# A chunked delta rule: inverses by row operations on VectorE instead of doubling on TensorE, state accumulated in PSUM, selected rows fetched by an indirect DMA

## The chip, the cores and the metric

The kernel runs on one core of one Trainium2 chip. The metric is the device time of one execution in microseconds (us). Besides the times there is one profiled execution, whose trace gives each engine's instructions: TensorE (PE, and PEld for its weight loads), VectorE (DVE), ScalarE (ACT), GpSimd (POOL), and the DMA issues of SyncE (SP).

## The reference

Two blocks follow each other, all in fp32. The first is the delta rule for 4 batches, 8 heads, 768 tokens and head size 48:

```python
k_n = k / (np.linalg.norm(k, axis=-1, keepdims=True) + 1e-06)
for t in range(S):
    y[:, :, t] = q_t @ state
    v_old = kn_t @ state
    state = state + beta_t * outer(kn_t, v_t - v_old)
```

The second is a mixture of depths on x = y with the heads joined (4 x 768 x 384). Each token's score is x . w_gate; in each batch the 128 tokens with the highest scores get x + sigmoid(score) * (relu(x w1) w2), with an inner size of 1024; the other tokens keep x.

## The kernel before

Tokens are taken in chunks of 64. In a chunk, with kn the normalised keys, S the state ahead of it and L[t, s] = beta_s kn_t.kn_s for s < t:

```
W = (I + L)^-1 (V - kn S)      Y = Q S + strict(Q (beta kn)^T) W      S <- S + (beta kn)^T W
```

A step is one chunk of two batches: 16 heads, stacked two by two on the 128 partitions (8 pairs). There are 24 steps, 12 for the first two batches (a group), then 12 for the other two.

`invert(i)` does what needs no state: keys are normalised (ACT, DVE, POOL), keys and queries are turned by TensorE (p_t, L236), the two 64x64 Gram matrices of a head are formed (p_g, L246) and masked. The inverse T = (I + L)^-1 then comes by doubling (L272 to L287): for blocks of 2, 4, 8, 16 and 32, p_x = L T (L262, masked on DVE at L275), p_ttt and p_tt (L262) give the corrections to T^T and T, which DVE subtracts (L281, L285). Each product is 16 matmuls of 64x64; the trace shows two MATMUL instructions for each, as fp32 products have. `recur(i)` then does the part that needs the state: p_r = kn S (L306), the difference on DVE (L309), p_w = T r (L316), its copy by ACT (L320), p_s (L330) and its addition to the state on DVE (L333), and the outputs p_y (L348, L354). `depths(g, ...)` is the second block for a group: a ranking by counting on DVE, a selection matrix, gathering the selected rows by 36 matmuls a batch (L442), two layers (L455, L464) and an indirect DMA that adds the result to the output.

All of these are generators. A loop at the end of the program advances them in turn, so an inverse runs two steps ahead of its recurrence; depths(0) is spread among the steps of the second group, and depths(1) comes after everything else. The Tile framework fixes each engine's order of instructions when the program is built; an engine then runs them in that order.

## Time and profile before

| | us |
|---|---|
| median of 3 runs (lowest, highest) | 770.15 (770.09, 771.6) |
| span of the profiled execution | 769.4 |
| PE busy | 704.5 |
| DVE busy | 391.0 |
| POOL busy | 146.5 |
| ACT busy | 139.8 |

The profiled execution's span, from its first to its last instruction, lies 0.75 us below the median of the timed runs; nothing else lies around it. Busy times are sums over an engine's instructions without overlap. Matmuls are pipelined, so the mean duration of one MATMUL (some 220 ns) is a latency; what one costs in a stream is the busy time of its group divided by its count.

### The profile page before, as it was taken

Reading aid. Unit: us, or ns where it says so; the run is one execution under the profiler, and the core shown is the slowest. Engines: PE = TensorE matmul, PEld = TensorE weight load, DVE = VectorE, ACT = ScalarE, POOL = GpSimd, SP = SyncE. Lnnn points to the kernel's source line nnn. Section 1 sums busy time; section 2 is a strip of 40 time slices with the busy share of each in tenths; the row PEclk is TensorE's granted clock in tenths of the full one; section 3 lists DMA queues with packets and bytes.
Section 4 is the critical chain, followed back from the end, with each engine's and each line's share of the span. In section 5 each row is a group of like instructions: output and inputs, shape, how many; then the busy total and the mean of one; then the engine's idle time right before and its main releaser. Section 6 shows DMA issues by size and latency. Waiting matters only on the chain.

```text
span 769.4 us, 35403 instructions
## 1 busy us (share of the span) xinstructions
PE 704.5 (92%) x16740; PEld 649.5 (84%) x16740; DVE 391.0 (51%) x788; ACT 139.8 (18%) x283; POOL 146.5 (19%) x154
## 2 busy tenths in 40 slices
PE   3799999999999999999989999999999999983496
PEld 2689899999989999998888888889999999972484
DVE  3466555654655555555845942345554654546500
ACT  3022121221112112212113122111120111101011
POOL 5322022202220222113201120222121210101001
PEclk9999999999999999999979999999999999995679
DMA  7621111110211112202101110121110000000001
GB/s 123 190 45 34 35 34 35 45 34 14 54 24 35 34 25 43 44 14 50 28 13 23 33 23 13 27 50 23 29 35 9 24 4 3 24 3 22 0 1 20
DMA packets 82210, 25.38 MB, mean 33 GB/s; under 512 B 76944, under 2 KB 81680, under 8 KB 82064
## 3 DMA queue, kind: packets, MB, share of 16 engines
q1 hardware_dynamic: 81488, 22.33, 13.5%
q8 instruction: 131, 2.15, 1.2%
q0 software_dynamic: 576, 0.79, 0.8%
q14 instruction: 15, 0.12, 0.1%
HBM read 17.60 MB, written 5.51 MB: 30 GB/s over the span
## 4 chain that ended last, share of the span: by engine, by line
PE 80%; DVE 10%; DMA 3%; POOL 2%; issue 2%; ACT 1%; SPq 1%; POOLq 0%; ACTq 0%; DVEq 0%
PE p_ttt L262 15%; PE p_x L262 14%; PE p_tt L262 10%; PE p_t L236 5%; PE p_g L246 5%; PE p_y L354 4%; PE p_y L348 4%; DVE junk_r L410 4%; PE p_s L330 3%; PE p_m L455 3%; PE p_t L262 3%; PE p_w L316 3%; PE p_m L442 3%; PE p_r L306 3%; DMA k_raw<-in_k_dram 2%; PE p_m L464 2%
## 5 line engine op out<-in xcount | busy, mean ns | idle before, releaser
L262 PE MATMUL p_x<-tt,lt 64*64 64x64 f32 x3840 | 139.9, 222 | 9.5 <-DVE tt L285 8.5
L262 PE MATMUL p_ttt<-ttt,x 64*64 64x64 f32 x3840 | 139.9, 222 | 5.1 <-DVE x L275 4.8
L281 DVE TENSOR_TENSOR ttt<-ttt,p_ttt 128x512 f32<-128x512 f32 x120 | 82.4, 687 | 118.5 <-PE p_ttt L262 118.5
L262 PEld LDWEIGHTS p_x<-tt,lt 64*64 64x64 f32 x3840 | 124.5, 136 | 21.0 <-DVE tt L285 15.1
L262 PEld LDWEIGHTS p_ttt<-ttt,x 64*64 64x64 f32 x3840 | 123.6, 136 | 15.0 <-DVE x L275 7.5
L275 DVE TENSOR_TENSOR x<-lmask,p_x 128x512 f32<-128x512 f32 x120 | 82.4, 686 | 99.5 <-PE p_x L262 97.6
L262 PE MATMUL p_tt<-x,ttt 64*64 64x64 f32 x3072 | 106.9, 219 | 0.0
L262 PEld LDWEIGHTS p_tt<-x,ttt 64*64 64x64 f32 x3072 | 98.9, 136 | 0.0
L285 DVE TENSOR_TENSOR tt<-tt,p_tt 128x512 f32<-128x512 f32 x96 | 65.8, 685 | 16.8 <-PE p_tt L262 16.6
L220 POOL TENSOR_TENSOR kn<-k_raw,rn 128x384 f32<-128x384 f32 x24 | 19.9, 827 | 252.2 <-PE p_t L236 243.3
L320 ACT COPY wbd<-p_w 64x384 f32<-64x384 f32 x48 | 22.7, 473 | 160.7 <-PE p_w L316 160.1
L348 PE MATMUL p_y<-s,qt 48*64 48x48 f32 x704 | 48.9, 220 | 0.0
L223 POOL TENSOR_TENSOR bmask<-mask_u,beta_t 128x512 f32<-128x512 f32 x24 | 25.5, 1064 | 120.2 <-DVE pt L249 119.8
L348 PEld LDWEIGHTS p_y<-s,qt 48*64 48x64 f32 x704 | 45.1, 137 | 0.0
L354 PE MATMUL p_y<-wbd,pt 128*64 128x96 f32 x384 | 43.2, 255 | 1.1 <-ACT wbd L320 1.1
L255 POOL TENSOR_TENSOR ttt<-lt,m 128x512 f32<-128x512 f32 x24 | 33.9, 1410 | 27.5 <-DVE lt L249 27.5
L354 PEld LDWEIGHTS p_y<-wbd,pt 128*64 128x64 f32 x384 | 33.7, 138 | 4.8 <-ACT wbd L320 1.2
L237 ACT COPY kt<-p_t 48x512 f32<-48x512 f32 x48 | 25.6, 578 | 62.9 <-PE p_t L236 62.9
L226 POOL TENSOR_TENSOR kb<-kn,beta_t 128x384 f32<-128x384 f32 x24 | 19.9, 828 | 89.4 <-PE p_s L330 89.2
L330 PE MATMUL p_s<-wbd,kb 128*48 128x96 f32 x352 | 34.1, 249 | 0.0
L333 DVE TENSOR_TENSOR s<-s,p_s 48x384 f32<-48x384 f32 x40 | 21.8, 546 | 23.0 <-PE p_s L330 20.8
L364 DVE CUSTOM_DVE_ANT_0 junk<-x,wg 128x384 bf16<-128x384 f32 x24 | 23.1, 964 | 20.1 <-ACT x L361 20.1
(95 smaller groups left out, 833.7 us busy)
## 6 DMA issues: line engine op xcount, KB each, us to landing
k_raw<-in_k_dram SPq DMA_DIRECT2D x48, 96.0 KB, 3.0
q_raw<-in_q_dram SPq DMA_DIRECT2D x48, 96.0 KB, 3.0
v_raw<-in_v_dram SPq DMA_DIRECT2D x48, 96.0 KB, 2.9
out_dram<-x SPq DMA_DIRECT2D x24, 192.0 KB, 1.9
w_sb<-in_moe_w_dram SPq DMA_DIRECT2D x2, 1536.0 KB, 12.1
wg<-in_moe_w_gate_dram SPq DMA_DIRECT2D x1, 192.0 KB, 6.1
beta_sb<-in_beta_dram SPq DMA_DIRECT2D x2, 48.0 KB, 2.7
out_dram<-oe,idx POOLq DMA_INDIRECT x4, 4.4
```

The source lines that it names most:

```text
L236: nc.tensor.transpose(ps[:D, r * P:(r + 1) * P], x[:, r0 + r], ident)
L237: nc.scalar.copy(xt[:, r0:r0 + 4].rearrange("d r t -> d (r t)"), ps[:D])
L246: nc.tensor.matmul(ps[hs, r], lhsT=kt[:, r, hs], rhs=x[:, r, hs], start=True, stop=True)
L255: nc.gpsimd.tensor_tensor(out=ttt, in0=lt, in1=bc(m1), op=ALU.mult)
L262: nc.tensor.matmul(ps[hs, r], lhsT=lhsT[hs, r], rhs=rhs[hs] if rhs is ident2 else rhs[hs, r], start=True, stop=True)
L275: nc.vector.tensor_tensor(out=x, in0=bc(lmask[s]), in1=ps, op=ALU.mult)
L281: nc.vector.tensor_tensor(out=new, in0=ttt, in1=ps_a, op=ALU.subtract)
L285: nc.vector.tensor_tensor(out=new, in0=tt, in1=ps_b, op=ALU.subtract)
L330: nc.tensor.matmul(ps[:, r], lhsT=m["kb"][:, bb * HP + r], rhs=wb[:, bb * HP + r], start=True, stop=True)
L348: nc.tensor.matmul(y[rows, h * D:(h + 1) * D], lhsT=m["qt"][:, r, par * C:(par + 1) * C], rhs=s_old[:, r, par], start=(h == 0), stop=False ...
L354: nc.tensor.matmul(y[rows, r * 2 * D:(r + 1) * 2 * D], lhsT=m["pt"][:, bb * HP + r], rhs=wb[:, bb * HP + r], start=(c == 0 and r == 0), st ...
L410: nc.vector.tensor_scalar(out=junk[:, :e - a], in0=rows[:, a:e], scalar1=mine, scalar2=None, op0=op, op1=ALU.add, accum_out=count[:, j, o: ...
```

## The change

The part that needs no state is now `prep` for a chunk (a unit: still one chunk of two batches). Heads of the two batches sit at partitions 0 to 47 and 64 to 111 of kq and kn, padded to 64, so one transpose serves two heads, and matmuls of the two batches use different row halves of the PE array. Beta is no longer folded into keys but into the inverse.

The inverse is now made for four chunks at once (`eliminate(e)`, six calls). The 64x64 matrices are split in half; each 32x32 diagonal block becomes one partition's 1024 numbers (128 blocks, 128 partitions) through a DVE transpose, and DVE inverts all of them with 30 row operations of two instructions each, on (31 - j) x j elements for j = 1 to 30. `join(e)` then makes the lower left quarter by two products of 32x32 blocks (p_z, p_j), copied by ACT. Two SBUF to SBUF DMAs a unit and two a call put blocks where they are needed. Calls of `eliminate` for the next four chunks are advanced among the units.

In `recur` the state stays in PSUM over all chunks of a group (p_s): the new product accumulates there, and ACT copies the sum out. The score of a token is now formed by a product on POOL and a sum on ACT. In `depths` the selected rows come by an indirect DMA from the output and three transposes a batch instead of 36 matmuls. Loads of k, q and v are cut in four DMAs instead of two, and beta is read by 96 small DMAs, issued on ACT's queue ahead of ACT's first computation. Eight units are prepared and the first call of `eliminate` is finished before the first recurrence.

The diff, cut to its core (removed lines are mostly those of the functions above):

```diff
+    BC = 4
+    NB = BC * GP
+    NE = NG * NCH // BC
+    assert NB == HC
+    DP = 64
...
+    KB = 3
+    qraw = [const.tile([P, HP, GB, DP], FP32, name=f"q_raw{m}") for m in range(KB)]
+    NKN = 9
+    kns = [const.tile([P, HP, GB, DP], FP32, name=f"kn{m}") for m in range(NKN)]
+        g, c = units[i]
+        if name == "q":
+            t = qraw[i % KB]
...
+            for bb in range(GB):
+                r0 = (g * GB + bb) * HP
+                nc.sync.dma_start(
+                    out=dst[par * C:(par + 1) * C, bb],
+                    in_=src[name][par, c * C:(c + 1) * C, r0:r0 + HP])
...
+    for g in range(NG):
+        for e in range(NCH // BC):
+            for par in range(2):
+                for half in range(2):
+                    for c in range(BC):
+                        p0 = (par * 2 + half) * HC + c * GP
+                        for r in range(1):
+                            nc.scalar.dma_start(
+                                out=bt[p0:p0 + GP, g * (NCH // BC) + e],
+                                in_=beta_src[par, half, g, e, c])
+    nbt = const.tile([P, NE, HC], FP32, name="nbt")
...
+    def prep(i):
+        g, c = units[i]
+        e, m = divmod(i, BC)
...
+        kn = kns[i % NKN]
+        for bb in range(GB):
+            nc.gpsimd.tensor_tensor(
+                out=kn[:, :, bb, :D], in0=kr[:, bb], op=ALU.mult,
+                in1=rn[:, bb * HP:(bb + 1) * HP, None].to_broadcast([P, HP, D]))
+        yield
+        kq = keep.tile([P, HP, 2, P], FP32, name="kq")
+        for o, x in ((1, qr), (0, kn)):
+            ps = ps_inv("p_t")
+            for r in range(HP):
+                nc.tensor.transpose(ps[:, r * P:(r + 1) * P],
+                                    x[:, r].rearrange("p b d -> p (b d)"), ident)
+            nc.scalar.copy(kq[:, :, o], ps.rearrange("p (r t) -> p r t", t=P))
+            yield
+        ps = [ps_inv("p_g").rearrange("p (r t) -> p r t", t=P) for bb in range(GB)]
+        for r in range(HP):
+            for bb, par in order:
+                ds = slice(bb * DP, bb * DP + D)
+                hs = slice(par * C, (par + 1) * C)
+                nc.tensor.matmul(ps[bb][hs, r], lhsT=kq[ds, r, 0, hs],
+                                 rhs=kq[ds, r, :, hs], start=True, stop=True)
+        pt = keep.tile([P, HP, GB, C], FP32, name="pt")
+        gv = gs[e][:, m * GP:(m + 1) * GP].rearrange("p (r b) t -> p r b t", b=GB)
+        for bb in range(GB):
+            nc.scalar.copy(gv[:, :, bb], ps[bb][:, :, :C])
+            nc.vector.tensor_tensor(
+                out=pt[:, :, bb], in0=ps[bb][:, :, C:], op=ALU.mult,
+                in1=mask_u[:, None, :].to_broadcast([P, HP, C]))
+        for par in range(2):
+            hs = slice(par * C, par * C + HC)
+            ms = slice(m * GP, (m + 1) * GP)
+            nc.sync.dma_start(out=gs[e][hs, ms, HC:], in_=gs[e][hs, ms, :HC])
+        made[i] = dict(kn=kn, kq=kq, pt=pt)
+    def eliminate(e):
+        gt = gs[e]
+        a = work.tile([P, HC, HC], FP32, name="a")
+        tmp = work.tile([P, HC * HC // 4], FP32, name="a_tmp", bufs=1)
+        nc.vector.transpose(out=a, in_=gt[:, :, HC:].rearrange("p n t -> p t n"))
+        yield
+        nc.vector.tensor_tensor(out=a, in0=a, op=ALU.mult,
+                                in1=nbt[:, e, :, None].to_broadcast([P, HC, HC]))
+        nc.gpsimd.affine_select(out=a, in_=a, pattern=[[1, HC], [-1, HC]], base=0,
+                                channel_multiplier=0, compare_op=ALU.is_gt, fill=0.0)
+        nc.gpsimd.memset(a.rearrange("p i c -> p (i c)")[:, ::HC + 1], 1.0)
+        yield
+        for j in range(1, HC - 1):
+            w = HC - 1 - j
+            t = tmp[:, :w * j].rearrange("p (i c) -> p i c", c=j)
+            nc.vector.tensor_tensor(
+                out=t, op=ALU.mult,
+                in0=a[:, j + 1:, j:j + 1].to_broadcast([P, w, j]),
+                in1=a[:, j:j + 1, :j].to_broadcast([P, w, j]))
+            nc.vector.tensor_tensor(out=a[:, j + 1:, :j], in0=a[:, j + 1:, :j],
+                                    in1=t, op=ALU.add)
+            yield
+        nc.vector.tensor_tensor(out=a, in0=a, op=ALU.mult,
+                                in1=bt[:, e, None, :].to_broadcast([P, HC, HC]))
+        yield
+        tt = tts[e % NTT]
+        nc.vector.transpose(out=tt[:, :, HC:].rearrange("p n t -> p t n"), in_=a)
+        for par in range(2):
+            hs = slice(par * C, par * C + HC)
+            nc.sync.dma_start(out=tt[hs, :, :HC], in_=tt[hs, :, HC:])
+        yield
+        nc.vector.transpose(out=gt[:, :, HC:].rearrange("p n t -> p t n"),
+                            in_=a.rearrange("p i c -> p c i"))
+        yield
+        yield from join(e)
+    def join(e):
+        gt, tt = gs[e], tts[e % NTT]
+        for m in range(0, BC, 2):
+            n0 = m * GP
+            lo = [slice(par * C, par * C + HC) for par in range(2)]
+            hi = [slice(par * C + HC, (par + 1) * C) for par in range(2)]
+            ns = slice(n0, n0 + 2 * GP)
+            ps = ps_inv("p_z").rearrange("p (n t) -> p n t", t=HC)
+            for b in range(2 * GP):
+                for par in range(2):
+                    nc.tensor.matmul(
+                        ps[lo[par], b], lhsT=gt[hi[par], n0 + b, :HC],
+                        rhs=tt[hi[par], n0 + b, HC:], start=True, stop=True)
+            for par in range(2):
+                nc.scalar.activation(gt[lo[par], ns, :HC], ps[lo[par]], AF.Copy,
+                                     scale=-1.0)
+            yield
+            ps = ps_inv("p_j").rearrange("p (n t) -> p n t", t=HC)
+            for b in range(2 * GP):
+                for par in range(2):
+                    nc.tensor.matmul(
+                        ps[lo[par], b], lhsT=gt[lo[par], n0 + b, HC:],
+                        rhs=gt[lo[par], n0 + b, :HC], start=True, stop=True)
+            for par in range(2):
+                nc.scalar.copy(tt[lo[par], ns, HC:], ps[lo[par]])
...
+    p_s = psum.tile([P, HP, 2 * D], FP32, name="p_s")
+    nc.vector.memset(p_s, 0.0)
...
+        ps = psum.tile([P, 2, 512], FP32, name="p_r", tag="rec", bufs=1)
+        pr = ps[:, :, :HP * D].rearrange("p b (r d) -> p b r d", d=D)
+            for r in range(HP):
+                for bb, par in order:
+                    ds = slice(bb * DP, bb * DP + D)
+                    hs = slice(par * C, (par + 1) * C)
+                    nc.tensor.matmul(pr[hs, bb, r], lhsT=kq[ds, r, 0, hs],
+                                     rhs=s_old[ds, r, par], start=True, stop=True)
...
-            s_new = state.tile([D, GP, 2, D], FP32, name="s")
-            for bb in range(GB):
-                ps = ps_rec("p_s")[:D, :HP * 2 * D].rearrange(
-                    "p (r h d) -> p r h d", h=2, d=D)
-                rs = slice(bb * HP, (bb + 1) * HP)
-                for r in range(HP):
-                    nc.tensor.matmul(ps[:, r], lhsT=m["kb"][:, bb * HP + r],
-                                     rhs=wb[:, bb * HP + r], start=True, stop=True)
-                if c > 0:
-                    nc.vector.tensor_tensor(out=s_new[:, rs], in0=s_old[:, rs],
-                                            in1=ps, op=ALU.add)
-                else:
-                    nc.vector.tensor_copy(s_new[:, rs], ps)
+            for r in range(HP):
+                for bb in range(GB):
+                    nc.tensor.matmul(p_s[bb * DP:bb * DP + D, r],
+                                     lhsT=kn[:, r, bb, :D],
+                                     rhs=wb[:, bb, r].rearrange("p h d -> p (h d)"),
+                                     start=(c == 0 and r == 0), stop=True,
+                                     skip_group_check=True)
+            s_new = sts[i % 2]
+            nc.scalar.copy(s_new.rearrange("p r h d -> p r (h d)"), p_s)
...
+                xw = work.tile([P, DM], FP32, name="xw", bufs=1)
+                nc.gpsimd.tensor_tensor(out=xw, in0=xj, in1=wg, op=ALU.mult)
+                nc.scalar.activation(junk, xw, AF.Copy,
+                                     accum_out=tok[b][:, j, 1:2])
...
+            xe = moe.tile([CAP, DM], FP32, name="xe")
+            nc.gpsimd.indirect_dma_start(
+                out=xe, out_offset=None, in_=out_flat[:(b + 1) * S, :],
+                in_offset=bass.IndirectOffsetOnAxis(ap=idx[b][:, 0:1], axis=0))
+            xes[b] = xe
+            yield
+        for b in bs:
+            ps = ps_inv("p_m")
+                nc.tensor.transpose(ps[:, t * CAP:(t + 1) * CAP],
+                                    xes[b][:, t * P:(t + 1) * P], ident[:CAP, :CAP])
...
-                for j in range(NT):
-                    nc.tensor.matmul(ps[:, t * CAP:(t + 1) * CAP],
-                                     lhsT=xs[b][:, j, t * P:(t + 1) * P],
-                                     rhs=sel[b][:, j],
-                                     start=(j == 0), stop=(j == NT - 1))
...
+    for i in range(BC):
+        start_prep(i)
+        if i == 1:
+            load_weights()
+        finish("prep")
+    ensure(0, "v")
+    ensure(1, "v")
+    running["elim"] = eliminate(0)
+    for i in range(BC, 2 * BC):
+        start_prep(i)
+        for _ in range(8):
+            advance("prep")
+            advance("elim")
+        finish("prep")
+    finish("elim")
+    TICKS = 10
+    for i in range(n):
+        e, m = divmod(i, BC)
+        if m == 0:
+            finish("elim")
+            if e + 1 < NE:
+                running["elim"] = eliminate(e + 1)
+        ensure(i + 2, "v")
+        running["rec"] = recur(i)
+        if i == NCH:
+            running["moe"] = depths(0)
+        start_prep(i + 2 * BC)
```

## Rows read from the trace of the kernel before

**Rows 1.** The page's busy times: engine, busy us (share of span), instructions
```profile
PE 704.5 (92%) x16740; PEld 649.5 (84%) x16740; DVE 391.0 (51%) x788; ACT 139.8 (18%) x283; POOL 146.5 (19%) x154
```

**Rows 2.** Three stretches: us; busy us of PE, PEld, DVE, ACT, POOL; PEclk; DMA
```profile
20.00:40.00 20.00, 15.11 (x305) 13.83 (x303) 9.03 (x17) 2.48 (x6) 6.83 (x7) 1.00 0.59 170
...
100.00:200.00 100.00, 99.84 (x2688) 94.25 (x2685) 54.37 (x96) 18.96 (x40) 18.68 (x19) 1.00 0.16 33
...
680.00:700.00 20.00, 14.39 (x280) 12.20 (x274) 6.72 (x12) 3.70 (x7) 2.72 (x2) 0.81 0.06 22
```

**Rows 3.** Groups of PE instructions: shapes, count | busy us, mean ns | idle
```profile
L262 PE MATMUL p_x<-tt,lt 64*64 64x64 f32 x3840 | 139.9, 222 | 9.5 <-DVE tt L285 8.5 <-ACT tt L269 0.7
...
L262 PE MATMUL p_tt<-x,ttt 64*64 64x64 f32 x3072 | 106.9, 219 | 0.0
...
L348 PE MATMUL p_y<-s,qt 48*64 48x48 f32 x704 | 48.9, 220 | 0.0
...
L354 PE MATMUL p_y<-wbd,pt 128*64 128x96 f32 x384 | 43.2, 255 | 1.1 <-ACT wbd L320 1.1
L330 PE MATMUL p_s<-wbd,kb 128*48 128x96 f32 x352 | 34.1, 249 | 0.0
...
L236 PE MATMUL p_t<-ident,q_raw 128*48 128x128 f32 x192 | 26.2, 281 | 3.3 <-DVE beta_t L170 3.3
...
L455 PE MATMUL p_m<-xeT,w_sb 128*128 128x256 f32 x96 | 23.1, 389 | 0.6 <-ACT xeT L446 0.6
...
L464 PE MATMUL p_m<-w_sb,hT 128*128 128x384 f32 x64 | 21.3, 489 | 0.0
```

**Rows 4.** Groups of DVE, ACT and POOL instructions, same columns
```profile
L281 DVE TENSOR_TENSOR ttt<-ttt,p_ttt 128x512 f32<-128x512 f32 x120 | 82.4, 687 | 118.5 <-PE p_ttt L262 118.5
...
L364 DVE CUSTOM_DVE_ANT_0 junk<-x,wg 128x384 bf16<-128x384 f32 x24 | 23.1, 964 | 20.1 <-ACT x L361 20.1
...
L320 ACT COPY wbd<-p_w 64x384 f32<-64x384 f32 x48 | 22.7, 473 | 160.7 <-PE p_w L316 160.1
...
L237 ACT COPY qt<-p_t 48x512 f32<-48x512 f32 x48 | 25.5, 578 | 25.6 <-PE p_t L236 25.5
...
L220 POOL TENSOR_TENSOR kn<-k_raw,rn 128x384 f32<-128x384 f32 x24 | 19.9, 827 | 252.2 <-PE p_t L236 243.3 <-DVE rn L216 8.9
...
L211 DVE TENSOR_REDUCE rn<-ksq 128x8 f32<-128x384 f32 x24 | 13.2, 549 | 9.6 <-ACT ksq L209 9.5
...
L423 DVE TENSOR_TENSOR sel<-iota_r,rank 128x768 f32<-128x768 f32 x4 | 3.8, 958 | 0.1
```

**Rows 5.** Timeline, two p_x products of 32 instructions: start us, us
```profile
26.50 1.97 PE L262 MATMUL p_x<-tt,lt 64*64 64x64 f32 x32 [0.68 <-ACT tt L269]
...
33.73 1.15 PE L262 MATMUL p_x<-tt,lt 64*64 64x64 f32 x32 [0.79 <-DVE tt L285]
```

**Rows 6.** DMA issues: a load pair in the timeline, the stores, the indirect ones
```profile
30.71 1.27 SPq L96 DMA_DIRECT2D k_raw<-in_k_dram  x2
...
L362 SPq DMA_DIRECT2D out_dram<-x x24: 332/338/572, 97.5 to 694.5; - x24
...
DMA to landing us min/median/max: 1.9/1.9/4.2
...
out_dram<-oe,idx POOLq DMA_INDIRECT x4, 4.4
```

**Rows 7.** Timeline at the recurrence's end and in the tail
```profile
691.67 2.27 PE L354 MATMUL p_y<-wbd,pt 128*64 128x96 f32 x16 [1.12 <-ACT wbd L320]
...
693.85 1.47 POOL L379 TENSOR_TENSOR diag<-ident,tok 128x768 f32<-128x768 f32 x1 [34.82 <-DVE tok L364]
...
694.49 1.25 DVE L364 CUSTOM_DVE_ANT_0 junk<-x,wg 128x384 bf16<-128x384 f32 x1 [0.71 <-ACT x L361]
...
713.03 5.77 PE L442 MATMUL p_m<-sel,x 128*128 128x128 f32 x36
...
734.71 6.82 PE L442 MATMUL p_m<-sel,x 128*128 128x128 f32 x36
```

More of the change, by code (lines that the diff above doesn't have):

```diff
@@ L17 @@
 C = 64
+HC = 32
 @with_exitstack
@@ L156, in bc @@
[L156 to L160 removed]
+    mask_u = const.tile([P, C], FP32, name="mask_u")
+    for par in range(2):
+        hs = slice(par * C, (par + 1) * C)
+        nc.gpsimd.affine_select(out=mask_u[hs], in_=ones[hs, :C], pattern=[[1, C]],
+                                base=0, channel_multiplier=-1,
+                                compare_op=ALU.is_gt, fill=0.0)
@@ L173 @@
+    tts = [const.tile([P, NB, C], FP32, name=f"tt{m}") for m in range(NTT)]
+    for t in tts:
+        nc.gpsimd.memset(t, 0.0)
     iota_r = const.tile([P, CAP], FP32, name="iota_r")
@@ L287, in invert @@
             yield
-        made[i] = dict(kb=kb, kt=kt, qt=qt, pt=pt, ttt=ttt)
-    xs, st_g, p_y = {}, {}, {}
+    st_g, p_y = {}, {}
+    p_s = psum.tile([P, HP, 2 * D], FP32, name="p_s")
+    nc.vector.memset(p_s, 0.0)
+    sts = [const.tile([P, HP, 2, D], FP32, name=f"s{m}") for m in range(2)]
     def recur(i):
-        g, c = steps[i]
+        g, c = units[i]
+        e, ch = divmod(i, BC)
         m = made.pop(i)
+        kq, kn, pt, tt = m["kq"], m["kn"], m["pt"], tts[e % NTT]
         vr = raw.pop((i, "v"))
@@ L472, in depths, with advance @@
             yield
-    def ps_alone():
-        return psum.tile([P, 512], FP32, name="p_m", tag="m", bufs=1)
-    HALF = 9
-    AHEAD = 2
-    n = len(steps)
-    load(0, "v")
-    for i in range(1, AHEAD + 1):
-        for name in "kqv":
-            load(i, name)
-    load_weights()
-    running = {}
-    def advance(key):
-        gen = running.get(key)
-        if gen is not None and next(gen, running) is running:
-            del running[key]
+    running = {}
+    def advance(key, times=1):
+        for _ in range(times):
+            gen = running.get(key)
+            if gen is not None and next(gen, running) is running:
+                del running[key]
     def finish(key):
```

283 lines of the change are left out of this document (88 added, 195 removed).

## The prediction, made before the changed kernel was run

> **What bounds the kernel now.** I read the page's busy times first, then stretches by the window, then the groups of instructions, last the timeline of the end. PE is busy 704.5 of 769.4 us and DVE half as long [rows 1]. In the stretch from 100 to 200 us PE is busy 99.84 of 100 us at a granted clock of 1.00 [rows 2]: a step there costs what its matmuls cost, and waits of others are covered. Most of PE's time is the doubling: p_x 139.9 us, p_ttt as much with the same count, p_tt 106.9 [rows 3]. That is 36 ns an instruction; the 768 of the first transpose (p_t, L262) at this price are 28 more. So 415 of the 704.5 us belong to work that the change takes from TensorE.
>
> The pace of PE can be read closer in the timeline: 32 instructions of one product span 1.15 us, the last one's own latency of 0.22 included, so one starts every (1.15 - 0.22) / 31 = 30 ns; at 26.5 us the same product took 1.97 us, 56 ns each [rows 3, 5]. These products alternate between two quarters of the array. Where consecutive matmuls stay in one quarter the price is 48.9 / 704 = 70 ns (p_y, L348, 48 columns); with 96 columns and all 128 rows it is 97 (p_s) to 112 ns (p_y, L354) [rows 3].
>
> The end matters too: the last output product ends at 691.67 + 2.27 = 693.9 us, and 75.5 us of second block follow with nothing beside them [rows 7].
>
> **The change: PE's share of a unit.** All fp32 products are two instructions each, transposes one.
> - Turning keys and queries: 8 instructions instead of 16, 26.2 / 192 = 0.136 us each [rows 3]: 1.1 us.
> - Gram products: 32 instructions instead of 64, 128 columns wide. No row shows this form. From below each costs the pace of 30 ns: 1.0 us. From above I extend the line from 70 ns (48 columns) to 112 (96 columns) to 140 ns at 128 columns and let two run side by side: 2.2 us. I take 1.7, since the four quarters are all used.
> - p_r and p_w: 32 each at 30 ns, 1.0 us each.
> - p_s: 16, now in two column halves of the array in turn: between 16 x 97 = 1.55 us [rows 3] and half of it, 0.8. I take 1.0.
> - p_y from the state: 32, now alternating row halves within one column half: 1.0 (30 ns) to 2.2 us (70 ns), I take 1.5. p_y from W: 16 x 112 ns, 1.8 us, as before.
> - join: 256 instructions in four units, 64 x 30 ns = 1.9 us.
>
> Low, taken, high: 9.7, 11.0, 12.8 us a unit, where 769.4 us now hold 24 steps. The trace shows two quarters in turn at 30 ns against 70 in one [rows 3, 5]. [...]
>
> **DVE's share.** Two groups give its price: 512 elements 687 ns, 768 elements 958 ns [rows 4], so 1.06 ns an element and 145 ns fixed. The row operations are 60 instructions on 2 x 4960 elements: 60 x 0.145 + 9920 x 0.00106 = 19.2 us. Three transposes and two products of 1024 elements are 1.23 us each at this price (transposes on DVE have no row; below, half of it, above, twice): 6.2. One call is 25.4 us, 6.35 a unit. prep adds 0.55 (the reduce, [rows 4]), three small ones and two masks of 256 elements: 1.85; the difference in recur 0.55. Together 8.75 us. What goes: five levels of three instructions of 0.69 us.
>
> To this comes POOL. The score's product on DVE reads two SBUF operands; by the price above 384 elements are 0.55 us, but its mean is 0.96 [rows 4], and at 694.49 it took 1.25 us beside POOL's diag, which ran from 693.85 to 695.32 [rows 7]. All row operations have two SBUF operands. POOL's work in a unit is 2 x 0.41 for kn (half of L220 each, [rows 4]), 0.83 for the score and a quarter of one select of 1024 elements (2.2 us at L220's price): 2.2 us. DVE is thus at 8.75 to 11 us a unit, nearly even with PE. ACT has some six instructions of 0.5 us more than one step had, and stays at about 6 us.
>
> **The chain of the recurrence in a unit:** p_r 1.15, difference 0.55, p_w 1.15, two copies of 0.47 in turn [rows 4], p_s 1.0 to 1.55, one copy of 0.5 for the state: 5.7 to 6.3 us with hops. It is covered as long as PE has prep and join to do.
>
> So neither PE (11) nor DVE (up to 11) nor the chain (6) fills a unit alone; instructions don't yield to each other, and orders are fixed beforehand. I take 13 us for the 16 units with a prep beside them, 9.5 for the four with only an eliminate (PE 8.2, DVE 8.3), 7.5 for the last four (chain 6, PE 6.3). 208 + 38 + 30 = 276. depths(0) adds its two layers to PE, (23.1 + 21.3) / 2 = 22 us [rows 3]: 298 us. With 11 us a unit where I take 13 (and 8 and 6.5 later) it would be 256.
>
> **The start**, which has no cover. ACT issues 96 DMAs ahead of its first computation. SP's issue of a load (512 pieces) takes 1.27 / 2 = 0.64 us, that of a store (128 pieces) 0.34 [rows 6]; one of 8 pieces lies on that line at 0.24. Ends 23 and 61 us; I take 0.34: 32, with the first instruction and a landing of 1.9 us [rows 6] ACT begins at 35 us. Behind it waits the first Square and so everything. The first prep: about 2.6 us of small steps on ACT, DVE and POOL, 4.5 on PE at the slow pace [rows 5], 1.3 for copies, 3 for the DMA of the block: 11.5. Three more behind it at PE's 4.5: 25 in all. Then the first eliminate, 25.4 plus 2.2 for POOL's select, with four preps' 1.85 on the same DVE: 35. Then join for the first two units, two products of 64 instructions at 56 ns and two copies of 0.58 each time [rows 4, 5]: 9.5. The recurrence begins at 105 us. Two loads in place of one on SP cost nothing here: they hide behind ACT's issues; without that cover they'd be 0.34 us each.
>
> **The tail.** 75.5 us now. The two groups of gather matmuls go, 5.77 us ahead of the second batch's ranking and 6.82 ahead of the layers [rows 7]. In place of the second stand an indirect DMA (4.4 us from issue to landing for those of before, [rows 6]) and three transposes, 5.2 us; the first is covered by the second batch's ranking. The score goes through POOL and ACT, 0.8 us more than DVE alone. PE will have waited for the gather and starts the layers at the slow pace of [rows 5]: I add 2.5 us, between nothing and the 8 us that the first layer's 11.5 us would cost more at 1.7 times the price. 75.5 - 12.6 + 5.2 + 0.8 + 2.5 = 71 us. Stores and gathers of the same rows are ordered by DMA waits, which fall on POOL's and SP's queues while these have nothing else.
>
> **Sum:** 105 + 298 + 71 = 474 us of span, with the 0.75 between span and median 475 us.
>
> **Rivals.**
> 1. *Waits bind the unit.* DVE's row operations stand in a fixed order with the difference that the recurrence waits for, and PE waits with it. At 17 us a unit (12 and 10 later, 30 for depths(0)) the middle is 390 us, the total 567. For it: three engines within 11 us of each other, each also waiting for another. Against: the present program keeps PE at 99.84 of 100 us with as many hand-overs [rows 2].
> 2. *The slow clock.* From 680 to 700 us PE was busy 14.39 of 20 us and the granted clock was 0.81; from 20 to 40 it was busy 15.11 us, with p_x still at 1.97 us at 26.5 [rows 2, 5]. PE at 11 of 13 us is not far above. At 1.97 / 1.15 = 1.7 times PE's price a unit is some 21 us (15 and 12 later, 38 for depths(0)): 482, total 661. Against: at that pace PE would be busy nearly all the time, as from 100 to 200 us, where the clock was 1.00. [...]
> 3. *Slower than before: row operations that wait for POOL each time.* If E is one eliminate, the total is (80 + E) + (5 E + 73) + 72, with E once in the start and five times bound by DVE. It passes 770 at E = 91 us, when a row operation costs (91 - 6) / 60 = 1.4 us instead of 0.32. That is what the score's product paid beside a running POOL instruction [rows 7], for every one of 60; but POOL works 2.2 us in a unit.
>
> **Chances:** forecast 0.60 (417 to 555: start 92 to 135, middle 256 to 340, tail 68 to 79), rival 1 0.20, rival 2 0.15, rival 3 0.05. The range 420 to 625 leaves out most of rivals 2 and 3 and the forecast's lowest edge. A change under 0.2% is about what a measurement of this kernel can't tell from none: faster 0.95, within it 0.01, slower 0.04.
>
> **What would show it.** ACT's first Square at about 35 us; the first p_w at 105; DVE's row operations at 0.32 us on average; p_x, p_ttt, p_tt gone and PE at some 340 us; units 13 us apart up to the 16th; p_g below 70 ns an instruction; about 71 us from the last p_y to the end. Wrong if ACT's issues cost twice as much, if PE's clock falls in the middle, or if DVE idles ahead of the difference while PE idles behind it.

## The result and the profile after

The changed kernel takes 534.86 us (median of 4, 534.48 to 538.1) against 770.22 (median of 4) for the kernel before: ratio 0.694, 95% interval 0.6912 to 0.6969. Its profiled span is 532.8 us. The first two lines are the page's busy times of the changed kernel, the third TensorE's granted clock in 40 slices.

```profile
PE 322.5 (61%) x5652; PEld 273.4 (51%) x5652; DVE 264.5 (50%) x722; ACT 166.8 (31%) x378; POOL 84.6 (16%) x126
...
PEclk9999999555569959965975576699969758856599
```

PE has lost 382 of the 704.5 us of [rows 1], but it is no longer the engine that everything waits for: 61% busy, and its granted clock, 1.00 where [rows 2] show the doubling, is mostly between 0.5 and 0.9 in a slice. Stretches of the changed kernel follow: one for each of the start's phases (first four), then one for each block of four units (the fourth block, which holds depths(0), in two), the last for the tail. At the start PEclk can't be taken at its word: a stretch from 75 to 85 us shows 1.00, although the 32 instructions of p_g took 1.98 us at 77.8 and 83.7, and 1.10 at 88.5.

```profile
core 0: us, PE busy (x) PEld busy (x) DVE busy (x) ACT busy (x) POOL busy (x), PEclk, DMA share, GB/s
0.00:70.00 70.00, 1.09 (x4) 0.72 (x4) 0.63 (x4) 0.67 (x1) 8.68 (x30) 1.00 0.31 77
70.00:99.00 29.00, 17.15 (x200) 12.73 (x200) 9.18 (x33) 14.63 (x35) 5.75 (x12) 0.92 0.27 48
99.00:140.00 41.00, 13.58 (x182) 10.13 (x180) 38.68 (x98) 9.37 (x23) 6.25 (x10) 0.50 0.35 62
140.00:151.00 11.00, 9.11 (x229) 8.26 (x229) 10.07 (x33) 5.23 (x10) 0.00 (x0) 0.50 0.10 18
...
151.00:194.00 43.00, 38.39 (x914) 34.22 (x914) 26.82 (x57) 21.61 (x51) 9.78 (x14) 0.86 0.40 79
194.00:247.00 53.00, 44.06 (x959) 38.98 (x960) 36.69 (x91) 25.50 (x60) 9.23 (x12) 0.79 0.37 73
247.00:306.00 59.00, 43.64 (x844) 37.48 (x841) 35.77 (x94) 23.84 (x55) 12.52 (x16) 0.70 0.33 66
306.00:356.00 50.00, 34.37 (x538) 30.34 (x537) 43.61 (x156) 18.75 (x39) 7.64 (x10) 0.73 0.20 44
356.00:389.00 33.00, 31.89 (x418) 24.61 (x418) 10.18 (x12) 13.36 (x31) 8.21 (x7) 0.98 0.25 43
389.00:435.00 46.00, 34.29 (x856) 31.91 (x854) 28.87 (x67) 15.60 (x34) 4.43 (x6) 0.72 0.19 43
435.00:458.00 23.00, 18.40 (x399) 17.40 (x398) 1.66 (x3) 7.47 (x18) 2.00 (x2) 0.84 0.06 20
458.00:533.00 75.00, 36.50 (x128) 26.64 (x126) 22.31 (x80) 10.78 (x25) 10.11 (x8) 0.72 0.08 16
```

For 70 us no engine works on the tokens; POOL fills constants for 8.7 us. The timeline of ACT says why: 96 issues of 0.71 us stand ahead of its first Square.

```profile
0.80 68.50 ACTq L138 DMA_DIRECT2D bt<-in_beta_dram  x96
69.33 1.28 ACT L195 ACT_TABLE_LOAD   x1 [69.33 <-DMA bt<-in_beta_dram]
70.62 0.53 ACT L195 ACTIVATE ksq<-k_raw 128x384 f32<-128x384 f32 x1
```

The parts of an elimination (groups of DVE's instructions, six calls in all): row operations, transposes, products.

```profile
L256 DVE TENSOR_TENSOR a_tmp<-a 128x30 f32<-128x30 f32 (+9 forms) x180 | 67.3, 374 | 6.7 <-POOL a L249 2.8
L260 DVE TENSOR_TENSOR a<-a,a_tmp 128x30 f32<-128x30 f32 (+9 forms) x180 | 64.2, 357 | 4.4
...
L273 DVE STREAM_TRANSPOSE g<-a 128x1024 f32<-128x1024 f32 x6 | 12.6, 2105 | 0.0
...
L245 DVE STREAM_TRANSPOSE a<-g 128x1024 f32<-128x1024 f32 x6 | 11.6, 1930 | 2.0 <-DMA g<-g 1.9
L267 DVE STREAM_TRANSPOSE tt<-a 128x1024 f32<-128x1024 f32 x6 | 11.5, 1918 | 0.1
...
L247 DVE TENSOR_TENSOR a<-a,nbt 128x1024 f32<-128x1024 f32 x6 | 7.3, 1222 | 0.1
```

Last, one border between blocks in the timeline: the third elimination begins (L245), its second transpose (L267) ends at 231.2, TensorE, idle 3.2 us for it, starts the join (p_z), SP issues the shift, and ACT copies the next unit's W (L344) at 247.6; the unit before had that copy at 222.0.

```profile
188.98 1.92 DVE L245 STREAM_TRANSPOSE a<-g 128x1024 f32<-128x1024 f32 x1
...
229.27 1.91 DVE L267 STREAM_TRANSPOSE tt<-a 128x1024 f32<-128x1024 f32 x1
...
231.23 1.92 PE L288 MATMUL p_z<-tt,g 32*32 32x32 f32 x64 [3.23 <-DVE tt L267]
...
233.24 1.34 SPq L270 DMA_DIRECT2D tt<-tt  x2
...
247.62 0.96 ACT L344 COPY wbd<-p_r 64x384 f32<-64x384 f32 x2 [1.04 <-PE p_r L339]
```

Of the 25.6 us of this border 9.2 pass before the join can begin and 16.4 behind it. The first line below is that second part: TensorE is busy for 13.6 of 16.6 us, at a granted clock of 0.50, with the join and with the next preparation's p_t and p_g, which stand ahead of the rest of the unit's p_r in its order. The second line is the same part of the third border, whose join began at 288.9 behind 10.8 us of waiting.

```profile
231.00:247.60 16.60, 13.63 (x317) 12.30 (x319) 6.38 (x8) 6.84 (x13) 0.00 (x0) 0.50 0.46 93
290.00:306.00 16.00, 13.37 (x265) 10.57 (x260) 3.06 (x9) 6.84 (x13) 1.47 (x1) 0.50 0.41 84
```

The profile also gives the chain of work that ended last, followed back from the last instruction to what released each step. Its shares of the whole span:

```profile
PE 39%; DVE 25%; issue 17%; ACT 7%; POOL 5%; DMA 4%; SPq 2%; POOLq 0%; DVEq 0%; ACTq 0%
```

Between the first and the last unit's copy of W (305 us) TensorE has 163 us of this chain, DVE 87 (45 of them row operations), ACT 30, and SP's queue and the DMAs together 4.

These copies mark the units. In the table, "first" is the first unit's copy, "middle" the time from there to the last unit's, "by blocks" the middle cut into blocks 1 to 3, block 4 (with depths(0)) and blocks 5 and 6, each up to the next block's first copy, and "borders" the steps from the last copy of a block to the first of the next (inside a block the changed kernel's are mostly 9 us, or 7 in the last two blocks; the fourth border lies in depths(0)). All runs of the experiments stand here; their times are of one run each, all_edits apart (a median of four; its copies are those of the profiled run). Four runs of the changed kernel lie within 3.6 us of each other and four of all_edits within 5.0, so a single run that differs by less than some 5 us shows neither gain nor loss.

| kernel | us | first | middle | by blocks (1 to 3, 4, 5 and 6) | borders |
|---|---|---|---|---|---|
| changed kernel | 534.86 | 151.1 | 304.8 | 155.1, 83.0, 66.7 | 16.1, 25.6, 31.2, 33.3, 23.0 |
| beta_late | 509.2 | 105.0 | 325.8 | 175.2, 83.2, 67.3 | 28.5, 31.7, 36.9, 25.1, 22.4 |
| beta_64 | 513.3 | 130.5 | 304.5 | 154.2, 83.4, 66.9 | 15.5, 25.5, 31.2, 34.3, 23.0 |
| elim_twice | 578.6 | 152.6 | 347.5 | 172.0, 102.4, 73.1 | 12.6, 28.0, 32.2, 51.7, 29.7 |
| no_rows | 487.3 | 135.6 | 273.2 | 150.1, 70.3, 52.9 | 24.6, 22.6, 28.8, 33.6, 7.9 |
| no_state_reads | 535.2 | 153.0 | 303.7 | 147.9, 87.9, 67.8 | 14.8, 28.2, 33.3, 36.6, 22.1 |
| kv_halved | 532.5 | 150.2 | 303.2 | 153.3, 82.2, 67.7 | 15.7, 25.6, 31.2, 32.9, 23.0 |
| shift_off_sp | 528.6 | 152.9 | 297.0 | 142.9, 88.6, 65.5 | 13.3, 24.0, 16.1, 44.3, 23.1 |
| one_more_buffer | 531.2 | 152.7 | 300.1 | 150.5, 85.0, 64.7 | 15.9, 21.7, 33.2, 36.0, 20.6 |
| state_in_sbuf | 535.4 | 150.2 | 306.6 | 154.6, 85.8, 66.3 | 15.9, 25.5, 30.1, 35.2, 22.5 |
| one_unit_earlier | 527.9 | 150.7 | 297.7 | 152.9, 93.9, 51.0 | 12.3, 14.4, 25.3, 17.0, 8.0 |
| beta_and_sp | 463.6 | 94.1 | 290.8 | 137.8, 86.6, 66.4 | 17.8, 19.0, 20.0, 39.3, 22.4 |
| all_edits | 467.6 | 102.5 | 283.6 | 136.0, 97.1, 50.4 | 12.0, 8.8, 7.7, 48.0, 8.0 |

### The profile page after: what moved, and what is told of

Same layout as the page of the kernel before. It is cut to its first block, busy times and chain, and to the rows that moved or that the text cites. A ratio compares the mean times of both kernels' runs of the same rounds, so it can differ in the third digit from the quotient of the medians.

```text
span 532.8 us, 13538 instructions
## 1 busy us (share of the span) xinstructions
PE 322.5 (61%) x5652; PEld 273.4 (51%) x5652; DVE 264.5 (50%) x722; ACT 166.8 (31%) x378; POOL 84.6 (16%) x126
## 4 chain that ended last, share of the span: by engine, by line
PE 39%; DVE 25%; issue 17%; ACT 7%; POOL 5%; DMA 4%; SPq 2%; POOLq 0%; DVEq 0%; ACTq 0%
DVE a_tmp L256 5%; PE p_y L376 5%; DVE a L260 5%; DVE junk_r L435 5%; PE p_m L483 4%; PE p_r L339 4%; PE p_j L298 4%; PE p_s L350 3%; PE p_m L492 3%; PE p_t L214 3%; PE p_z L288 3%; PE p_g L223 3%; PE p_y L369 2%; DMA k_raw<-in_k_dram 2%; PE p_m L416 2%
## 5 line engine op out<-in xcount | busy, mean ns | idle before, releaser
L256 DVE TENSOR_TENSOR a_tmp<-a 128x30 f32<-128x30 f32 (+9 forms) x180 | 67.3, 374 | 6.7 <-POOL a L249 2.8
L260 DVE TENSOR_TENSOR a<-a,a_tmp 128x30 f32<-128x30 f32 (+9 forms) x180 | 64.2, 357 | 4.4
L206 POOL TENSOR_TENSOR kn<-k_raw,rn 128x192 f32<-128x192 f32 x48 | 26.1, 565 | 209.2 <-PE p_s L350 76.7
L339 PE MATMUL p_r<-r,tt 64*64 64x48 f32 x704 | 33.0, 241 | 16.8 <-DVE r L329 14.4
L376 PEld LDWEIGHTS p_y<-wbd,pt 128*64 128x64 f32 x384 | 40.7, 162 | 3.0 <-ACT wbd L344 1.9
L223 PE MATMUL p_g<-kq 48*64 48x128 f32 x768 | 37.6, 327 | 7.1 <-ACT kq L216 7.1
L339 PEld LDWEIGHTS p_r<-r,tt 64*64 64x64 f32 x704 | 29.0, 154 | 19.7 <-DVE r L329 16.3
L388 POOL TENSOR_TENSOR xw<-x,wg 128x384 f32<-128x384 f32 x24 | 25.0, 1042 | 88.6 <-ACT x L385 79.8
L344 ACT COPY wbd<-p_r 64x384 f32<-64x384 f32 x48 | 22.7, 473 | 50.0 <-PE p_r L339 37.4
L216 ACT COPY kq<-p_t 128x512 f32<-128x512 f32 x48 | 27.4, 586 | 32.4 <-PE p_t L214 30.1
L223 PEld LDWEIGHTS p_g<-kq 48*64 48x64 f32 x768 | 28.9, 163 | 12.8 <-ACT kq L216 10.6
L369 PE MATMUL p_y<-s,kq 48*64 48x48 f32 x704 | 31.8, 231 | 0.0
L298 PE MATMUL p_j<-g 32*32 32x32 f32 x768 | 25.2, 230 | 8.4 <-ACT g L292 8.3
```

What stands on the lines that cost most here:

```text
L216: nc.scalar.copy(kq[:, :, o], ps.rearrange("p (r t) -> p r t", t=P))
L223: nc.tensor.matmul(ps[bb][hs, r], lhsT=kq[ds, r, 0, hs], rhs=kq[ds, r, :, hs], start=True, stop=True)
L256: nc.vector.tensor_tensor(out=t, op=ALU.mult, in0=a[:, j + 1:, j:j + 1].to_broadcast([P, w, j]), in1=a[:, j:j + 1, :j].to_broadcast([P, w, ...
L260: nc.vector.tensor_tensor(out=a[:, j + 1:, :j], in0=a[:, j + 1:, :j], in1=t, op=ALU.add)
L298: nc.tensor.matmul(ps[lo[par], b], lhsT=gt[lo[par], n0 + b, HC:], rhs=gt[lo[par], n0 + b, :HC], start=True, stop=True)
L339: nc.tensor.matmul(pw[hs, bb, r], lhsT=tt[hs, ch * GP + r * GB + bb], rhs=rhs[hs, bb, r], start=True, stop=True)
```

## The experiments

Two questions were open: what an issue of a DMA costs at the start, and what fills the borders.

**beta_64 and beta_late: the start.**

```diff
-    out=bt[p0:p0 + GP, g * (NCH // BC) + e], in_=beta_src[par, half, g, e, c]   # 96
+    out=bt4[p0:p0 + GP - 1:GB, g], in_=beta_r[par, half, c, g, bb]              # 64
```

> The same bytes in the same pieces (768 of 128 bytes), all still on ACT's queue ahead of the first Square, but as 64 loads of 12 pieces in place of 96 of 8. If an issue has a price of its own (0.71 us whatever it carries), the last issue ends at 0.8 + 64 x 0.71 = 46 us, the first Square starts near 48 and the time falls by 23 us to 512. If the price is by the piece (0.089 us each), both stay at 70 and 535.

The 64 issues took 47.56 us, 0.74 each, the first Square came at 49.7, and the gain was 21.5 us, 20.6 of them by the first unit's copy. The price is by the issue here and not by the piece: 0.74 us with 12 pieces, 0.71 with 8. SP's loads of k agree (second line, from kv_halved): 512 pieces in one issue took 0.64 us, as 256 do in the changed kernel. Not every issue has this price, though: SP's stores took a median of 0.34 us before and of 0.39 in the changed kernel (0.33 to 1.61), its two loads of w_sb 0.4; what makes the difference was not tested.

```profile
0.80 47.56 ACTq L140 DMA_DIRECT2D bt<-in_beta_dram  x64
...
212.74 1.27 SPq L111 DMA_DIRECT2D k_raw<-in_k_dram  x2
```

```diff
-    (96 loads of beta on nc.scalar, one activation for all of nbt)
+    load_bt(0, nc.scalar)            # 16, ahead of the first Square
+    load_bt(e, nc.sync)              # 16 each, a block or two ahead of use
```

> Of the 96 loads of beta at the head of ACT's queue the 16 of the first elimination stay there; the other 80 go to SP's queue, 16 after the first four preparations and 16 in each of the next four blocks, and the sign change is made for one elimination at a time. In the changed kernel's trace the 96 issues take 0.80 to 68.5 us, 0.71 us each, and the first Square starts at 70.6. Theory (the head of the kernel is the issuing of these loads on ACT, in front of everything ACT does for the preparations): the first Square starts near 16, the first elimination near 99 - 55 = 44, and as nothing behind it is changed the whole gain is kept: 480 us. Rival (the loads of k, q and the weights are late as well, or the blocks behind wait for something else): the first Square is early, but the first elimination starts only some 20 us sooner, and the time is 510 or more. Second rival (80 issues on SP cost there what they cost on ACT, and SP's loads of v, k and q come late): the middle grows by up to 57 us, and the time is near 535.

The first Square came at 13.4, the first unit's copy 46 us earlier, at 105.0, but only 25.7 us are left at the end. The timelines of SP, DVE, TensorE and ACT in this run show where part of the 21 went (the first border: 28.5 us in place of 16.1):

```profile
121.91 10.84 SPq L137 DMA_DIRECT2D bt<-in_beta_dram  x16
132.87 2.66 SPq L112 DMA_DIRECT2D v_raw<-in_v_dram  x4
...
131.04 1.98 DVE L267 STREAM_TRANSPOSE tt<-a 128x1024 f32<-128x1024 f32 x1
...
153.04 1.34 SPq L270 DMA_DIRECT2D tt<-tt  x2
...
156.14 0.45 PE L339 MATMUL p_r<-r,tt 64*64 64x48 f32 x2 [4.18 <-ACT tt L302]
...
155.51 2.13 ACT L302 COPY tt<-p_j 32x512 f32<-32x512 f32 x4 [1.55 <-DMA tt<-tt]
```

SP issues 16 loads for 10.84 us and everything behind them is late, the shift of tt too: it was issued at 153.0, though the transpose ahead of it ended at 133.0, and ACT's copy, which needs it, began at 155.5. The first three blocks grew by 20 us, the rest by less than 1. That is the second rival of the expectation, at a good third of its size.

**elim_twice, no_rows and no_state_reads: what paces the blocks.**

```diff
-            advance("elim")
+            advance("elim", 2)
```

> Two steps of the elimination are put out in each of a unit's ten places instead of one, so that an elimination is spread over two units of a block and not over four. In the changed kernel's trace the copies that end a unit's first product are 8.7 to 9.2 us apart inside a block and 16.1, 25.6, 31.2, 33.3 and 23.0 apart over the borders of blocks. Theory (the border is the elimination's last steps and its join, put out behind the block's last unit; the elimination takes 40 to 54 us because its steps stand in DVE's order behind work of units that is not there yet): eliminations take 30 us, their joins fall into the third unit, the border steps fall to about 11 us at the three borders without depths, and the time falls by 40 to 495. Rival (TensorE at its granted clock bounds the block: 44 of 53 us busy in the second): what the border loses the units gain, and the time moves by less than 10 us. Second rival (denser row operations on DVE delay the units' own subtraction): units get slower, 540 or more.

Slower by 44 us: the theory fell. The third elimination still took 42 us (204.7 to 247.1, against 44), though two of its steps stand in each place, and it began 16 us later. The join is now put out in the middle of a block and TensorE waits there: between 160 and 340 us it waits 22.7 us for the second transpose ahead of p_z (14.0 in the changed kernel). Block 4 alone grew by 19 us, which these waits don't explain.

```diff
-            nc.vector.tensor_tensor(out=t, op=ALU.mult, ...)
-            nc.vector.tensor_tensor(out=a[:, j + 1:, :j], ..., in1=t, op=ALU.add)
             yield
```

> Leaves out the 60 row operations of each elimination (so the inverses are not computed; every other instruction stays). In the changed kernel's trace an elimination's row operations take 21.9 us of DVE, and an elimination 40 to 54 us from its first transpose to its last. Theory (the elimination sets the first product's time and each border of blocks): the first unit comes 20 us sooner, the five borders lose about 15 us each, together 95 us, and the time is near 440. Rival (TensorE bounds the blocks): only the 20 us of the first elimination go, and the time is near 513.

47.6 us less, between the two: 15.5 at the start and 32 in the middle, but of these only 5 in the first three blocks, whose borders did not shrink together; 13 fell in block 4 and 14 in the last two. In the second block the elimination was over at 196.8, yet the next unit's copy came at 231.9 (timelines of DVE, SP and ACT):

```profile
192.33 1.97 DVE L261 STREAM_TRANSPOSE tt<-a 128x1024 f32<-128x1024 f32 x1
...
221.22 2.23 SPq L264 DMA_DIRECT2D tt<-tt  x2
...
227.96 0.37 ACT L228 COPY g<-p_g 128x256 f32<-128x256 f32 x1 [2.02 <-PE p_g L223]
228.23 2.13 ACT L296 COPY tt<-p_j 32x512 f32<-32x512 f32 x4
...
231.91 0.96 ACT L338 COPY wbd<-p_r 64x384 f32<-64x384 f32 x2 [1.55 <-PE p_r L333]
```

The shift was issued 27 us after its transpose had ended, behind SP's loads, but the trace shows nothing that waited for it: ACT's copy of the join into tt began straight behind its copy of the next preparation's Gram block, and that one had waited 2.0 us for p_g. SP spent 42.7 of this block's 47.6 us issuing (in the changed kernel 43.1 of 53.6), so its queue has little room left; yet of the chain between first and last copy (273 us) it has 4.6 us and the DMAs 10.7, against 178 of TensorE. In the first three blocks the row operations are thus not the pace: without them DVE falls from 43 to 10 us of the chain there, but ACT, POOL, SP's queue and the DMAs take 24 more, and TensorE keeps its 82 to 83.

```diff
-        if c > 0:
-            ... nc.tensor.matmul(p_y[bb][rows, ...], lhsT=kq[...], rhs=s_old[...]) ...
```

> Leaves out the products of q with the state in p_y (704 instructions, 31.8 us of TensorE between 151 and 459 us of the changed kernel's trace, none of them waited for), so that the output lacks that part; all else stays. Theory (TensorE, 80% busy in that stretch, paces the units as the prediction had it): the time falls by about as much as is left out, 25 to 32 us, to 506. Rival (the blocks are paced from border to border by the preparations, SP's queue, the elimination on VectorE and the join, with TensorE's work in their shadow): what is left out becomes idle time at the borders, and the time stays within 8 us of 535.

No gain (535.16): the amount of TensorE's work is not the pace, though its instructions make up half of the chain. What it no longer does became waiting. The first two lines are of the changed kernel (groups of TensorE), the next two the same groups in this run; the last number is the wait ahead of them.

```profile
L339 PE MATMUL p_r<-r,tt 64*64 64x48 f32 x704 | 33.0, 241 | 16.8 <-DVE r L329 14.4 <-ACT tt L302 2.2
L288 PE MATMUL p_z<-tt,g 32*32 32x32 f32 x768 | 22.3, 225 | 39.2 <-DVE tt L267 39.2
```

```profile
L339 PE MATMUL p_r<-r,tt 64*64 64x48 f32 x704 | 33.6, 248 | 24.6 <-DVE r L329 24.5
...
L288 PE MATMUL p_z<-tt,g 32*32 32x32 f32 x768 | 22.4, 224 | 45.1 <-DVE tt L267 44.7 <-issue 0.4
```

The units inside a block came 8 us apart in place of 9, and two of the first three borders grew by 2 us each: the first three blocks took 7 us less, block 4 took 5 more.

**kv_halved, shift_off_sp, one_more_buffer, state_in_sbuf: one cost at a time.**

```diff
-            for bb in range(GB): nc.sync.dma_start(out=dst[..., bb], ...)     # kv_halved: k and v
+            nc.sync.dma_start(out=t[...].rearrange("p b r d -> p (b r) d"), in_=src[...][..., g * GP:(g + 1) * GP])
-            nc.sync.dma_start(out=gs[e][hs, ms, HC:], ...)                    # shift_off_sp
+            nc.scalar.dma_start(out=gs[e][hs, ms, HC:], ...)
-            nc.sync.dma_start(out=tt[hs, :, :HC], ...)
+            nc.gpsimd.dma_start(out=tt[hs, :, :HC], ...)
-    keep bufs=8, NKN = 9                                                      # one_more_buffer
+    keep bufs=9, NKN = 10
-            nc.scalar.copy(s_new, p_s)                                        # state_in_sbuf
+            nc.vector.tensor_tensor(out=s_new, in0=s_old, in1=p_s, op=ALU.add)
```

> k and v of a unit are loaded with two issues each in place of four (the two batch rows of a load are one stretch of rows); same bytes and pieces. In the changed kernel's trace SP's queue is back to back through most of 160 to 260 us: a unit brings it 12 loads of some 0.65 us, 2 shifts of the Gram blocks, 0.65 each, and half a pair of stores, some 10.5 us, while units come 9 us apart inside a block; the shift of tt that the join of the second block needs is issued at 179.98 although the transpose in front of it ended at 171.8. Theory (SP's queue is what the blocks wait for: the shifts stand in it behind the loads): a unit's share falls by 4 x 0.65 = 2.6 us, four blocks lose 8 to 10 us each, and the time falls by 30 to 40, to 500. Rival (elimination and join, 44 + 16 us from border to border, set the pace alone): under 10 us.

2.4 us less, within what single runs differ by: the rival. SP's issuing fell from 43.1 to 31.6 us in the second block, and the block from 53.6 to 52.7.

> The two shifts that bring the halves of a block together go to other queues: that of the Gram blocks (g to g, two a unit) to ACT's, that of tt (two a block) to POOL's. Loads and stores stay on SP's. Theory (the shifts are late because they stand behind SP's loads): the elimination of a block starts some 9 us sooner and the shift of tt follows its transpose at once, so each of the first four borders loses 5 to 12 us, and SP loses 1.3 us a unit: the time falls by 25 to 45, to 500. Rival (the issue price, some 0.7 us, and ACT's or POOL's waits for the shifted data only move to those queues): within 10 us of 535.

6.2 us less, inside the rival's bound. But the first three blocks took 12 us less, most of it at the third border (31.2 to 16.1); the border behind it gave back 11 and block 4 took 6 more.

> kq and pt get nine buffers in place of eight and kn ten in place of nine, so that the preparation of unit i+8 no longer writes into the buffers of unit i while that is at work; the order of the instructions stays. In the changed kernel's trace VectorE waits 36.5 us for p_y before it writes pt (21.2 us in one place, ahead of the second group of units), and the row operations of the elimination stand behind that. Theory (these waits are part of the 40 to 54 us of an elimination): the time falls by 10 to 25, to 517. Rival (the waits are inside what the shifts and SP's queue cost anyway): within 5 us of 535.

3.7 us less, under the bound of the rival and within what single runs differ by.

> Undoes one part of the change: p_s starts anew in every unit and VectorE adds it to the state before, where the changed kernel accumulates in PSUM and ACT copies. VectorE gets 22 more operations of 128x384 at 0.54 us, 12 us in all, in the chain from unit to unit, ACT loses 22 copies of 0.48. Theory (the borders set the pace, and inside a block TensorE and SP's queue do): the time stays within 6 us of 535. Rival (the chain from unit to unit binds: the addition waits behind a row operation of the elimination, 0.4 us, and is no shorter than the copy): some 0.5 us a unit, 545.

0.6 us more: no share of the gain that this run could show comes from keeping the state in PSUM.

**one_unit_earlier, beta_and_sp, all_edits: together.**

```diff
-            if m == 0:       finish("elim"); running["elim"] = eliminate(e + 1)
+            if m == BC - 1:  finish("elim"); running["elim"] = eliminate(e + 2)
-        start_prep(i + 2 * BC)
+        start_prep(i + 2 * BC + 1)
```

> Every preparation is put out one unit earlier (unit i+9 beside unit i) and every elimination begins with the last unit of a block in place of the first of the next, with the buffers that this takes (kq and pt nine, kn ten, g three; a and ksq one, two tiles of the selection share one). In the changed kernel an elimination can't begin before the border, since the last preparation that it reads is put out beside the block's last unit; the block then takes its 40 to 54 us and the join (borders 16.1, 25.6, 31.2, 33.3, 23.0 us against 9 inside). Theory (elimination and join, from border to border, are the pace): the borders without depths fall to about 12 us, 10 to 18 us each, and the time falls by 25 to 40, to 502. Rival (SP's queue, some 10.5 us of issuing a unit, 43 a block and 1.4 for tt, is as slow by itself): the second and third blocks, 53.6 and 58.5 us, fall to some 47 at best, and the time falls by 10 to 17. Second rival (TensorE waits for the join in the middle of a block, as where two steps were put out at a time): 540 or more.

7 us less in all, neither the theory's 25 to 40 nor the rival's 10 to 17. All five borders fell, by 52 us together, but the units inside grew. By blocks: 2 us less in the first three, 16 less in the last two, 11 more in block 4, where depths(0) runs.

> Three edits together: beta in 64 loads of three eliminations each, of which 16 stay on ACT ahead of the first Square, 16 go to SP behind the first loads, and the 32 of the second half come five a unit on SP in units 0 to 6; k and v in two issues each; the two shifts on ACT's and POOL's queues. Theory (what 80 late loads of beta gave back, 21 of the 46 us won at the first product, was the shifts and loads that stood behind them on SP, a shift of tt issued at 153.0 behind a transpose that ended at 132.9): with SP lightened the 46 us are kept and the single gains, 2 and 6, come on top: 482. Rival (the borders are set by the elimination alone, which can't begin sooner than the preparations, and these by ACT and TensorE): the start is won and given back again at the first border, 505.

71 us less than the changed kernel, more than any theory had. The first unit came 57 us earlier and nothing was given back: in the first three blocks no engine waited more than 3.2 us for a DMA, where in beta_late POOL had waited 16.3 for k and DVE 5.4 for q. Which of the edits does that is not separated; SP has also only 48 loads of beta to issue, and not 80. The middle lost 14 us, where the two edits alone had lost 1.6 and 7.8; the first three blocks lost 17, where they alone had lost 2 and 12. These blocks:

```profile
94.00:140.00 46.00, 42.44 (x935) 37.77 (x934) 37.25 (x90) 23.82 (x56) 11.17 (x16) 0.84 0.36 75
140.00:185.00 45.00, 41.06 (x920) 36.19 (x920) 35.97 (x87) 23.83 (x57) 11.51 (x16) 0.80 0.47 93
185.00:232.00 47.00, 39.81 (x853) 33.78 (x852) 38.56 (x104) 24.25 (x58) 13.40 (x17) 0.79 0.42 82
```

46 us a block, with TensorE 40 to 42 and DVE 36 to 39 of them busy.

> The edits of the run before and the earlier preparations and eliminations together. Theory (start, SP's queue and the wait from border to border are three separate costs): 535 - 46 - 8 - 25 = 456. Rival (only one of SP's queue and elimination can be bound at a time, so that the second edit finds the other bound gone already): 480.

467.57 us (465.2 to 470.16), ratio to the kernel before 0.6059 (0.6004 to 0.6114): faster than both kernels, but not than the one run of beta_and_sp. In the middle the effects add up by blocks: 19 us less in the first three (17 and 2 alone), 16 less in the last two (0 and 16), 14 more in block 4 (4 and 11). Its first unit comes 8.4 us later than in beta_and_sp, behind one more preparation, although that preparation moved nothing in one_unit_earlier (150.7 for 151.1). Why block 4 grows in both runs whose eliminations begin earlier stays open.

## Why the prediction came out as it did

475 us were forecast (420 to 625), 534.86 measured: direction and range right, the span 59 us short (474 for 532.8). All three things that the prediction named as signs of being wrong came in part: ACT's issues cost twice as much, TensorE's clock fell in the middle, and DVE idled 38 us ahead of the difference (`r`), TensorE 14 behind it. By its steps:

- **The start, where 44 of the 59 us are.** First p_w at 105 us forecast, its main run began at 149.1. The step that failed is the price of ACT's 96 issues: taken at 0.34 us, measured 0.71 (first Square 70.6, not 35: 35.6 us). The line that was laid through two sizes of SP's issues [rows 6] towards few pieces does not hold; beta_64 shows a price by the issue: 8 and 12 pieces at 0.71 and 0.74 us on ACT's queue, and 256 and 512 at 0.64 on SP's, look the same. The other terms: preparations 28.4 us for 25, elimination 40.7 for 35, join 9.4 for 9.5.
- **The elimination**: 30.3 us of DVE's own instructions against 25.4. Row operations 131.5 / 6 = 21.9 (19.2; on average 0.365 us for 0.32), transposes 35.7 / 6 = 5.95 (3.7), products 1.22 (1.23). What the row operations took beyond their price is rival 3, small: 63 of the 360 ran beside a POOL instruction and took 13.4 us more in all than the shortest of their shape; without that an elimination's are at 19.7. Two of the same size, the first beside POOL's product of the score:

```profile
210.90 1.18 POOL L388 TENSOR_TENSOR xw<-x,wg 128x384 f32<-128x384 f32 x1 [0.73 <-ACT junk L390]
...
211.25 1.09 DVE L256 TENSOR_TENSOR a_tmp<-a 128x240 f32<-128x240 f32 x1
...
212.82 0.41 DVE L256 TENSOR_TENSOR a_tmp<-a 128x240 f32<-128x240 f32 x1
```

- **TensorE's share of a unit**: the groups of p_t, p_g, p_r, p_s, p_y, p_z and p_j sum to 282.0 us, 11.75 a unit (11.0 taken), 322.5 busy in all (340). p_g cost 37.6 / 768 = 49 ns an instruction, below the 70 named; turning keys and queries cost 1.74 us for 1.1.
- **The middle, right in size by another mechanism and with some luck.** 149.1 to 458.5 is 309 us; 298 were forecast. The first twelve units take 155.1 us, 12.9 each for 13; the block with depths(0) 83.0 (74), the next 46.0 (38), the end 23.3 (30). But units don't come 13 us apart, as the text had it, paced by three engines in turn: they come 9 us apart in fours, and 16 to 33 us pass at each border. No single engine was shown to set the pace: leaving out 31.8 us of TensorE's work brought nothing, leaving out the row operations 32 us of the middle, 5 of them in the first three blocks. The chain goes by turns through TensorE, DVE and ACT, and at a border through the end of an elimination, then the join and the next preparation. That is the mechanism of rival 1 (waits bind) at the forecast's size. The size owes something to luck: 13 us were 11 of TensorE and a margin that no row gave, and the slow clock, priced at nothing in the blocks, is in what was measured. SP's queue, 10.8 us of issuing a unit in the second block, was in no term: the prediction had the doubled loads hidden behind ACT's issues and looked no further. It has 4 us of the chain here, but late loads put on it cost 21.
- **What one total hides**: SP's edits (1.6 and 7.8 us of the middle) and earlier eliminations (7) looked small alone because block 4 gave back what other blocks won; by blocks their gains nearly add up. What still holds a block at 46 us in beta_and_sp, with TensorE at some 90% and DVE at 80%, was not settled.
- **Rival 2, the slow clock**, came in part: the mean granted clock was 0.70 to 0.86 in the first three blocks, and 0.50 behind TensorE's waits at two borders (3.2 us of waiting ahead of 231.2, 10.8 ahead of 288.9). Of TensorE's 163 us on the chain 94 lie in stretches at 0.50, the lower of the two levels in this trace (1.00 and 0.50). At the ratio of p_z's 1.92 and 1.20 us (below) they would take 59 at the upper one, so the clock cost up to some 35 us of the middle: an estimate from the chain, which no run tested. Rival 2's total adds up to 659 us, not 661, and the low value of TensorE's share to 9.6, not 9.7; neither changes anything.
- **The tail**: 458.5 to 532.8, 74.3 us for 71 and for 75.5 before. Fetching rows by an indirect DMA was not undone by itself, nor was the elimination on DVE put back for the doubling: that most of the gain comes from the 382 us that TensorE lost is read from the profiles.

## What to carry to other kernels

Count DMA issues, not their bytes: most cost their queue some 0.64 to 0.74 us here, in order, so the ones ahead of an engine's first instruction are start-up time, and late loads put in front of a small transfer that others wait for gave back 21 us. A busy share of 80% doesn't make an engine the bound; leaving out some of its work tells (31.8 us less of TensorE's brought nothing here). A late transfer isn't yet one that is waited for: look at what its reader waited for. And read a change by stages: one that wins 16 us in two blocks and loses 11 in another looks like 7.
